# State cross-attention, SiLU MLP and soft mixture of experts in one kernel: the first quarters of w_in laid out half behind half, block 1 moved between quadrants, constant products behind block 8, another order

## The chip, the cores and the metric

The kernel runs on one core of a Trainium2 chip. What counts is the device time of one execution in microseconds (us); the time of a kernel is the median of its runs.

## The reference, cut to what matters

```python
# x: 8 x 8 x 512 x 64, state: 8 x 8 x 32 x 64 (batch, head, rows, depth)
a = softmax(x @ state.T / 8);   xread = a @ state       # tokens read the state
a2 = softmax(state @ x.T / 8);  sread = a2 @ x          # the state reads the tokens
t = concat([xread, sread], rows) -> 4608 tokens x 512   # 8 x (512 + 32) rows

h = t @ w_in                      # 512 -> 2048
t = (h * sigmoid(h)) @ w_out      # 2048 -> 512

logits = t @ phi                  # 32 slots = 8 experts x 4
slot_input = softmax(logits, over tokens).T @ t         # 32 x 512
for e in range(8):                # w1: 512 -> 1024, w2: 1024 -> 512
    slot_out[e] = relu(slot_input[e] @ w1[e]) @ w2[e]
out = softmax(logits, over slots) @ slot_out            # 4608 x 512
```

w_in and w_out come as 64-bit numbers.

## The kernel before

Tokens are worked in nine blocks: blocks 0 to 7 have 512 tokens each (one batch of x), block 8 has the 256 state rows. Lines 1440 to 1750 only describe the work. Every operation is recorded by a `Recorder` (line 280), whose `schedule()` (line 467) plans an order for each engine from a cost model, the due place of each operation, and `RANK` (line 71), a table that shifts the due place of single kinds of operation by numbers; `issue()` (line 628) then issues all. So nearly every instruction has the line L628, and one goes by the names of the tiles.

The first 50 us are the **front**: 64-bit halves of w_in (`raw`, 1 MB each) land and `conv` (line 750) turns each into fp32. The steps are: a first ACTIVATE on ScalarE (ACT) makes the high word (`win<-raw`), a second one on ACT, or one on VectorE (DVE), the low word (`part`), DVE shifts (`TENSOR_SCALAR win`), and DVE or GpSimd (POOL) adds the two (`CUSTOM_DVE_ANT_0 win<-win,part`). `win_half` (line 793) does this for one half (256 columns of each of four 128-row chunks) of one quarter of w_in; a half's results lie in four pieces of 256 in the quarter's tile, so the two halves of a tile lie between one another.

For each block and each quarter of w_in, `wb_mm` (line 950) multiplies the state with that quarter on TensorE (PE): 16 matmuls of 64 rows (`wbp`), whose results are copied into a high and a low part (`wb`, two buffers, ACT, DVE and POOL). The token softmax (`e`, transposed by `eT`) then multiplies it: 16 tiles of hidden units per block (`h`, 6 matmuls each, `hid`, line 1020), SiLU (`g`), and the slot logits (`lg`, 32-column matmuls with w_out·phi, `w2p`). `sc`, `sr` and `srT` are the attention scores and the state's read for the next blocks. On `lg` follow the softmax over tokens (`d`, transposed by `dT`; `lT` transposes the logits) and the products `S` of the slots' weights with all of g (`s_dTg`, line 1259).

g lies for S with tokens on the partitions. DVE transposes each 32x32 square in place. In **moved** blocks (`MOVED`, line 28: blocks 2 to 6) the transposed squares go to one tile, `src`, and 4 DMAs per quarter of h (`by_tokens`, line 1002) carry them into `dst`, 16 DMAs of 256 KB per block; S is then 16 matmuls of 32x512 with all 128 rows, and `dT` is one transposition. In the others (0, 1 and 7) there is no DMA, S is 64 matmuls of 32 rows, and `dT` is four transpositions. Block 0 lies in `src`, block 1 in `dst`.

A scheduler window, `FILL` (line 61), has the planner put **constant products** on TensorE where it plans a gap of the first 60 us: `filler` (line 613) multiplies a tile of ones with itself into a free bank (`lg<-thb 128x256`, two instructions of the profile each). Nobody reads them.

`NATS` (line 22) says at which h of which block one half of w_out is converted and stored for the end (`wo_block`). Behind block 7 come `hid8` and `logits8` (block 8), the slots' sums (`dT`, `siT`, S, `si`), and then the experts: w1 (`f`), w2 (`so`, `sor`), the outputs (`o`). Their 32 weight loads of 1 MB, in `load_w` (line 1342), go from SyncE's queue into 24 `places`, tiles that come free; those in `PIECES` (line 1324) are loaded in four pieces of 256 KB.

Of the kernel before, what the change touches and what calls it, by code (L numbers as in the profile page):

```python
# [24 lines left out]
NATS = {1: {7: 0, 15: 1}, 3: {10: 2}, 4: {10: 3}, 5: {10: 4}, 6: {10: 5}}  # L25
# [5 lines left out]
MOVED = (2, 3, 4, 5, 6)  # L31
# [29 lines left out]
FILL = ((0.0, 60.0),)  # L61
# [10 lines left out]
    ("0", "ACT", "activation", "acc", 0): -711,  # L72
    ("0", "ACT", "activation", "acc", 6): 522,
    ("0", "ACT", "activation", "e", 1): 62,
    ("0", "ACT", "activation", "g", 1): 222,
    ("0", "ACT", "activation", "part", 0): -647,
    ("0", "ACT", "activation", "part", 6): 1417,
    ("0", "ACT", "activation", "win", 0): -724,
    ("0", "ACT", "activation", "win", 3): -17,
    ("0", "ACT", "activation", "win", 6): 1433,  # L80
    ("0", "ACT", "copy", "ar", 0): -198,
    ("0", "ACT", "copy", "e", 2): -428,
    ("0", "ACT", "copy", "e", 7): -578,
    ("0", "ACT", "copy", "wb", 3): 1386,
    ("0", "ACT", "copy", "wb", 5): 1379,
    ("0", "ACT", "copy", "ws", 2): 483,
    ("0", "ACT", "mul", "wp", 0): 1396,
    ("0", "DVE", "reciprocal", "asm", 0): 1500,
    ("0", "DVE", "reciprocal", "asm", 1): 1500,
    ("0", "DVE", "reciprocal", "tm", 0): -319,  # L90
    ("0", "DVE", "reduce_max", "tm", 0): -489,
    ("0", "DVE", "reduce_max", "tm", 1): -39,
    ("0", "DVE", "reduce_max", "tm", 2): 1381,
    ("0", "DVE", "reduce_sum", "tm", 1): -164,
    ("0", "DVE", "reduce_sum", "tm", 2): 1500,
    ("0", "DVE", "tensor_copy", "ss", 1): 643,
    ("0", "DVE", "tensor_scalar", "acc", 0): 1479,
    ("0", "DVE", "tensor_scalar", "acc", 4): -189,
    ("0", "DVE", "tensor_scalar", "acc", 5): -841,
    ("0", "DVE", "tensor_scalar", "asm", 3): 1500,  # L100
    ("0", "DVE", "tensor_scalar", "part", 1): -23,
    ("0", "DVE", "tensor_scalar", "part", 4): -1364,
    ("0", "DVE", "tensor_scalar", "tm", 0): -510,
    ("0", "DVE", "tensor_scalar", "win", 4): 599,
    ("0", "DVE", "tensor_tensor", "acc", 2): -30,
    ("0", "DVE", "tensor_tensor", "ar", 0): -504,
    ("0", "DVE", "tensor_tensor", "s", 0): -359,
    ("0", "DVE", "tensor_tensor", "s", 1): 2,
    ("0", "DVE", "tensor_tensor", "s", 2): 1500,
    ("0", "DVE", "tensor_tensor", "wb", 2): 719,  # L110
    ("0", "DVE", "tensor_tensor", "wb", 3): 387,
    ("0", "DVE", "tensor_tensor", "wb", 5): 1500,
    ("0", "DVE", "transpose", "s", 7): -1129,
    ("0", "DVE", "transpose", "src", 4): 1500,
    ("0", "PE", "matmul", "h", 11): -998,
    ("0", "PE", "matmul", "lg", 8): 1218,
    ("0", "PE", "matmul", "sr", 1): 1500,
    ("0", "PE", "matmul", "wps", 2): -662,
    ("0", "PE", "transpose", "eT", 2): 143,
    ("0", "SP", "dma_start", "phi", 0): 1486,  # L120
    ("0", "SP", "dma_start", "raw", 0): 3,
    ("0", "SP", "dma_start", "raw", 1): -2,
    ("0", "SP", "dma_start", "raw", 2): -4,
    ("0", "SP", "dma_start", "raw", 3): 229,
    ("0", "SP", "dma_start", "raw", 5): 1004,
    ("0", "SP", "dma_start", "raw", 6): 1497,
    ("0", "SP", "dma_start", "ss", 1): 1421,
    ("0", "SP", "dma_start", "xT", 0): -219,
    ("7", "ACT", "activation", "m", 0): 715,
    ("7", "ACT", "copy", "rd", 0): 199,  # L130
    ("7", "ACT", "copy", "wb", 0): -804,
    ("7", "DVE", "scalar_tensor_tensor", "acc", 2): -522,
    ("7", "DVE", "tensor_scalar", "m", 0): -587,
    ("7", "PE", "matmul", "h", 8): 110,
    ("7", "PE", "matmul", "lg", 0): 1500,
    ("7", "PE", "matmul", "lg", 12): 782,
    ("7", "PE", "matmul", "wbp", 1): 1332,
    ("7", "PE", "matmul", "wbp", 2): 488,
    ("8", "ACT", "activation", "cw", 0): 1042,
    ("8", "ACT", "copy", "dT", 1): -521,  # L140
    ("8", "DVE", "tensor_copy", "thb", 1): 272,
    ("8", "DVE", "tensor_scalar", "cm", 1): -1500,
    ("8", "PE", "matmul", "S", 0): 935,
    ("8", "PE", "matmul", "f", 0): -1213,
    ("8", "PE", "matmul", "f", 1): -790,
    ("8", "PE", "matmul", "f", 2): -693,
    ("8", "PE", "matmul", "f", 3): -899,
    ("8", "PE", "matmul", "f", 4): -1500,
    ("8", "PE", "matmul", "f", 5): -905,
    ("8", "PE", "matmul", "f", 6): -907,  # L150
    ("8", "PE", "matmul", "f", 7): -907,
    ("8", "PE", "matmul", "fold", 0): 1351,
    ("8", "PE", "matmul", "h", 0): 1101,
    ("8", "PE", "matmul", "h", 4): 99,
    ("8", "PE", "matmul", "h", 13): 622,
    ("8", "PE", "matmul", "h", 27): 395,
    ("8", "PE", "matmul", "lg", 4): 748,
    ("8", "PE", "matmul", "o", 3): -170,
    ("8", "PE", "matmul", "o", 5): 1500,
    ("8", "PE", "matmul", "o", 7): 420,  # L160
    ("8", "PE", "matmul", "o", 10): 568,
    ("8", "PE", "matmul", "so", 18): -257,
    ("8", "PE", "matmul", "so", 21): 1496,
# [36 lines left out]
    ("m", "DVE", "transpose", "dst", 2): -1188,  # L200
    ("m", "DVE", "transpose", "dst", 3): -1195,
    ("m", "DVE", "transpose", "dst", 5): 1238,
    ("m", "DVE", "transpose", "s", 0): -143,
    ("m", "DVE", "transpose", "s", 1): -68,
    ("m", "DVE", "transpose", "src", 2): -1448,
    ("m", "DVE", "transpose", "src", 3): -1500,
    ("m", "DVE", "transpose", "src", 4): 88,
    ("m", "DVE", "transpose", "src", 6): -1448,
    ("m", "DVE", "transpose", "src", 7): -1408,
    ("m", "PE", "matmul", "S", 0): 692,  # L210
    ("m", "PE", "matmul", "S", 1): 1286,
    ("m", "PE", "matmul", "S", 2): 1500,
    ("m", "PE", "matmul", "h", 1): 1487,
    ("m", "PE", "matmul", "h", 4): 1458,
    ("m", "PE", "matmul", "h", 6): 977,
    ("m", "PE", "matmul", "h", 10): 1104,
    ("m", "PE", "matmul", "h", 13): 889,
    ("m", "PE", "matmul", "lg", 0): 1500,
    ("m", "PE", "matmul", "lg", 1): 1500,
    ("m", "PE", "matmul", "lg", 3): 1500,  # L220
    ("m", "PE", "matmul", "lg", 6): 1064,
# [445 lines left out]
def tile_state_attention_soft_moe(  # L667
# [70 lines left out]
    def raw_at(n):  # L738
        return raws[0][:, n] if n < 4 else raws[1][:, n % 4]
# [280 lines left out]
    def hid(k, j):  # L1020
# [29 lines left out]
        if j == 0 and k < 2:  # L1050
            new_blk(("src", "dst")[k])
# [750 lines left out]
```

## Time and profile before

| | us |
|---|---|
| median of 3 runs | 442.78 (442.65 to 443.43) |
| profiled execution | 443.23 |
| its span | 441.4 |
| around the span | 1.8 |
| TensorE busy | 420.4 |
| VectorE busy | 291.4 |
| ScalarE busy | 284.6 |
| GpSimd busy | 117.6 |

The span runs from the first to the last instruction of the profiled execution. Busy time of TensorE is of pipelined matmuls with modelled ends. In the chain that ended last 84% of the span is TensorE, 6% DMA, 4% ACT.

### The profile page before, as it was taken

The page shows a single profiled execution, that of the slowest core. Times are in us where ns is not written, and L with a number is a line of the kernel's source. Part 1 is how long each engine was busy: PE and PEld are TensorE (multiplying, and loading weights), DVE is VectorE, ACT ScalarE, POOL GpSimd, SP SyncE. Part 2 cuts the span into 40 slices and gives each one's busy share as a digit, 9 for nine tenths or more (in the row PEclk, how much of TensorE's full clock was granted, in tenths as well). Part 3 has the DMA queues.
Part 4 walks back from the last instruction along what each step waited for, and adds up shares of the span by engine and source line. Part 5 has one row for each costly group of instructions (what it writes and reads, how often), then busy time and mean ns, then how long its engine had stood idle before and what let it go on. Part 6 is the DMA issues. An engine that isn't in the chain of part 4 may idle for free.

```text
span 441.4 us, 11019 instructions
## 1 busy us (share of the span) xinstructions
PE 420.4 (95%) x4577; PEld 273.4 (62%) x4577; DVE 291.4 (66%) x547; ACT 284.6 (64%) x512; POOL 117.6 (27%) x71
## 2 busy tenths in 40 slices
PE   7899999999999999999999999999999999999990
PEld 5565657757776775675687567578577684434440
DVE  3999999893797588569668847954865434321461
ACT  4799997757885577679867667766866535011360
POOL 0024332243253223434632511351352220000000
PEclk9999999999999999999999999999999998999996
DMA  8999832224336786998786767347699989999998
GB/s 312 429 423 423 335 145 97 98 97 107 138 143 164 220 262 148 287 316 235 234 227 205 170 204 191 89 120 185 207 415 348 343 318 374 385 425 426 389 329 290
DMA packets 36017, 113.10 MB, mean 256 GB/s; under 512 B 3200, under 2 KB 12288, under 8 KB 28032
## 3 DMA queue, kind: packets, MB, share of 16 engines
q1 hardware_dynamic: 35968, 112.41, 74.7%
q8 instruction: 36, 0.59, 0.5%
q14 instruction: 13, 0.11, 0.1%
HBM read 79.37 MB, written 12.06 MB: 207 GB/s over the span
## 4 chain that ended last, share of the span: by engine, by line
PE 84%; DMA 6%; ACT 4%; DVE 2%; issue 2%; SPq 0%; DVEq 0%
PE h L628 45%; PE S L628 8%; PE lg L628 7%; PE wbp L628 6%; DMA phi<-in_phi_dram 4%; PE so L628 3%; PE f L628 3%; DMA raw<-in_w_in_dram 2%; PE o L628 2%; PE eT L628 1%; PE sr L628 1%; PE sc L628 1%; PE gt L628 1%; ACT part L628 1%; PE w2ps L628 1%
## 5 line engine op out<-in xcount | busy, mean ns | idle before, releaser
L628 PE MATMUL h<-ar,wb 128*128 128x512 f32 x768 | 190.3, 400 | 0.5 <-ACT g L628 0.5
L628 PEld LDWEIGHTS h<-ar,wb 128*128 128x128 f32 x768 | 140.0, 188 | 48.6 <-ACT g L628 8.3
L628 DVE STREAM_TRANSPOSE src<-g 128x512 f32<-128x512 f32 x112 | 76.5, 698 | 24.0 <-ACT g L628 20.1
L628 ACT ACTIVATE g<-h 128x512 f32<-128x512 f32 x100 | 59.1, 609 | 25.9 <-PE h L628 19.7
L628 POOL TENSOR_TENSOR wb<-wf,wb 128x512 fp32r<-128x512 f32 x26 | 33.7, 1296 | 50.8 <-ACT wb L628 31.1
L628 POOL TENSOR_TENSOR s<-s,tm 128x1024 f32<-128x1024 f32 x12 | 23.3, 1938 | 69.3 <-DVE tm L628 19.8
L628 PEld LDWEIGHTS lg<-g,w2p 128*32 128x32 f32 x1056 | 27.2, 109 | 17.7 <-issue 12.8
L628 PE MATMUL lg<-g,w2p 128*32 128x128 f32 (+1 forms) x1056 | 37.0, 279 | 0.0
L628 ACT CAST wb<-wbp 128x512 fp32r<-128x512 f32 x64 | 35.4, 596 | 2.3 <-PE wbp L628 1.5
L628 PE MATMUL wbp<-win,ss 64*32 64x512 f32 x512 | 33.9, 599 | 1.5 <-DVE win L628 1.5
L628 DVE TENSOR_TENSOR wb<-wbp,wb 128x512 fp32r<-128x512 f32 x38 | 25.4, 676 | 12.4 <-ACT wb L628 12.2
L628 ACT ACT_TABLE_LOAD x21 | 26.9, 1283 | 1.1 <-PEq L1792 0.7
L628 DVE SCALAR_TENSOR_TENSOR g<-thb,h 128x512 f32<-128x512 f32 x28 | 18.6, 682 | 13.3 <-ACT thb L628 6.1
L628 ACT ACTIVATE thb<-h 128x512 f32<-128x512 f32 x30 | 18.0, 600 | 13.1 <-PE h L628 13.0
L628 PE MATMUL S<-dst,dT 128*32 128x512 f32 (+1 forms) x296 | 25.3, 608 | 0.0
L628 DVE SCALAR_TENSOR_TENSOR acc<-acc,m,S 128x512 f32<-128x512 f32 x28 | 20.1, 737 | 7.6 <-PE S L628 7.3
L628 PE MATMUL h<-wc,rd 128*128 128x512 f32 x96 | 24.1, 402 | 0.0
L628 PE MATMUL lg<-thb 128*128 128x256 f32 x80 | 20.7, 408 | 1.2 <-DVE thb L628 1.2
L628 POOL TENSOR_TENSOR src<-src 128x1024 uint32<-128x1024 uint32 x6 | 14.4, 2393 | 24.3 <-DVE src L628 24.3
L628 PEld LDWEIGHTS h<-wc,rd 128*128 128x128 f32 x96 | 17.5, 188 | 4.8 <-issue 1.0
L628 PEld LDWEIGHTS lg<-thb 128*128 128x128 f32 x80 | 15.7, 204 | 7.5 <-issue 4.2
L628 DVE TENSOR_REDUCE tm<-s 128x32 f32<-128x1024 f32 (+1 forms) x18 | 19.5, 1090 | 0.3 <-ACT s L628 0.2
(185 smaller groups left out, 604.6 us busy)
## 6 DMA issues: line engine op xcount, KB each, us to landing
dst<-src SPq DMA_DIRECT2D x80, 256.0 KB, 4.5
place<-in_w_dram SPq DMA_DIRECT2D x12, 1024.0 KB, 8.9
xT<-in_xT_dram SPq DMA_DIRECT2D x8, 1024.0 KB, 6.2
raw<-in_w_in_dram SPq DMA_DIRECT2D x8, 1024.0 KB, 10.6
raw<-in_w_outT_dram SPq DMA_DIRECT2D x8, 1024.0 KB, 8.2
xk<-in_xk_dram SPq DMA_DIRECT2D x8, 1024.0 KB, 7.4
src<-in_w_out_dram SPq DMA_DIRECT2D x6, 1024.0 KB, 7.2
dst<-in_w_dram SPq DMA_DIRECT2D x6, 1024.0 KB, 8.5
```

Source lines behind the costliest of these rows:

```text
L628: made = [call(*args, **kwargs) for call, args, kwargs in op.calls]
```

## The change

- `win_c` and `win_half`: quarters 0 and 1 of w_in (`BY_HALVES`) are laid out half behind half, 1024 numbers of a row each, so that each half is contiguous. `wb_mm` and `split_w` read a chunk as two pieces of 256.
- Block 1 is a moved block: it goes through `src` and 16 DMAs to `dst`; block 0 now lies in `dst` from the beginning.
- The halves of w_out in `NATS` are converted at other places.
- A second window of constant products, planned between 355 and 383 us, from the constants' tile `cst`.
- `('w', 1)`, the place of w_in's quarter 1, is loaded in one piece.
- `RANK` has other entries: 160 before, 118 now, 7 of them unchanged.

```diff
-NATS = {1: {7: 0, 15: 1}, 3: {10: 2}, 4: {10: 3}, 5: {10: 4}, 6: {10: 5}}
+NATS = {2: {13: 0}, 3: {10: 1}, 4: {10: 2}, 5: {6: 3, 14: 4}, 6: {10: 5}}
...
-MOVED = (2, 3, 4, 5, 6)
+BY_HALVES = (0, 1)
+MOVED = (1, 2, 3, 4, 5, 6)
...
-FILL = ((0.0, 60.0),)
+FILL = ((0.0, 60.0), (355.0, 383.0))
...
 RANK = {
-    ("0", "ACT", "activation", "acc", 0): -711,
+    ("0", "ACT", "activation", "acc", 2): -323,
...
-        out, v = self.tiles[name][:, 0:256], self.filling[0]
+        out, v = self.tiles[name][:, 0:256], self.filling[0 if start < 100 else 2]
...
+    def win_c(fq, c):
+        t = win_t[fq]
+        if fq not in BY_HALVES:
+            return t[:, c].rearrange("p (h f) -> p h f", h=2)
+        return t.rearrange("p c f -> p (c f)").rearrange("p (h c f) -> p c h f", h=2, c=4)[:, c]
+
     def win_half(fq, half):
         n = halves.index(("win", fq, half))
-        conv(raw_at(n), win_t[fq][:, :, 256 * half:256 * half + 256], share(half), n)
+        t = win_t[fq]
+        if fq in BY_HALVES:
+            t = t.rearrange("p c f -> p (c f)").rearrange("p (h c f) -> p c h f", h=2, c=4)[:, half]
+        else:
+            t = t[:, :, 256 * half:256 * half + 256]
+        conv(raw_at(n), t, share(half), n)
...
-                        rhs=win_t[fq][64 * h2:64 * h2 + 64, c, cols],
+                        rhs=win_c(fq, c)[64 * h2:64 * h2 + 64],
...
-        t = bufs["dst" if k == 1 else "src"]
+        t = bufs["dst" if k == 1 or (k == 0 and 1 in MOVED) else "src"]
...
-            new_blk(("src", "dst")[k])
+            new_blk(("src", "dst")[(k + (1 in MOVED)) % 2])
...
-        t, w = wc[n // 2 % 2][:, n % 2], win_t[fq][:, c]
+        t, w = wc[n // 2 % 2][:, n % 2].rearrange("p z (h f) -> p z h f", h=2), win_c(fq, c)
...
-    PIECES = (('w', 1), ('w', 2), ('w', 3))
+    PIECES = (('w', 2), ('w', 3))
...
-    nc.filling = thb[:, 0, 0:256], 1.5
+    nc.filling = thb[:, 0, 0:256], 1.5, cst[:, 0:256]
```

ScalarE in the front, from the first token softmax (`e_90`) to the first copies of `wb`, before; `win_78` is quarter 0 of w_in, `win_79` quarter 1, `raw` the landed halves, and the words in brackets are the semaphores waited for:

```order
L628 ACTIVATE e_90,asm_92<-e_90,asm_92 128x512 [waits DVE_49,Activation_49]
L628 ACTIVATE win_78<-raw_76 128x4x256 [waits DMAHW5_49,DVE_49]
L628 ACTIVATE part<-raw_76,ulps 128x1024
L628 COPY e_90<-eT_0_99 128x512 [waits PE_49]
L628 ACTIVATE acc<-raw_77 128x1024 [waits DMAHW6_49]
L628 ACTIVATE win_79<-raw_76 128x4x256 [waits DMAHW3_49]
L628 ACTIVATE part<-raw_76,ulps 128x1024 [waits DVE_49]
L628 CAST wb_94<-wbp_0_0_95 128x512 [waits PE_49]
```

The same place now:

```order
L588 ACTIVATE e_90,asm_92<-e_90,asm_92 128x512 [waits DVE_49,Activation_49]
L588 ACTIVATE win_78<-raw_76 128x1024 [waits DMAHW3_49]
L588 ACTIVATE part<-raw_76,ulps 128x1024
L588 ACTIVATE win_79<-raw_76 128x1024 [waits DMAHW5_49]
L588 ACTIVATE part<-raw_76,ulps 128x1024 [waits DVE_49,Activation_49]
L588 COPY e_90<-eT_0_99 128x512 [waits PE_49]
L588 ACTIVATE e_90,asm_92<-e_90,asm_92 128x512
L588 CAST wb_94<-wbp_0_1_96 128x512 [waits PE_49]
```

The second half of quarter 0 (`win_78`) waits for its landing alone, no longer for DVE too; quarter 1's first half comes directly behind it, and a conversion of w_out (`acc`) has gone from between.

TensorE in block 3, from `h_7` to `h_9`, before; `wbp` from `win_81` is this block's last quarter of w_in:

```order
L628 MATMUL h_7_367<-ar_298,wb_343 128x512 x6
L628 MATMUL lT_341<-cst,ls_337 128x128
L628 MATMUL S_0_0_362<-dst,dT_339 32x512 x4
L628 MATMUL lg_355<-g_2_348,w2p 32x128 x4
L628 MATMUL lg_355<-g_3_350,w2p 32x128 x4
L628 MATMUL lg_355<-g_4_352,w2p 32x128 x4
L628 MATMUL S_0_1_363<-dst,dT_339 32x512 x4
L628 MATMUL S_1_0_364<-dst,dT_339 32x512 x4
L628 MATMUL S_1_1_365<-dst,dT_339 32x512 x4
L628 MATMUL wbp_0_0_376<-win_81,ss 32x512 x4
L628 MATMUL wbp_0_1_377<-win_81,ss 32x512 x4
L628 MATMUL h_8_370<-ar_298,wb_356 128x512 x6
```

The same place now; `wbp` from `win_78` is the next block's first quarter:

```order
L588 MATMUL lT_341<-cst,ls_337 128x128
L588 MATMUL lg_355<-g_0_333,w2p 32x128 x4
L588 MATMUL S_0_0_362<-dst,dT_339 32x512 x4
L588 MATMUL S_0_1_363<-dst,dT_339 32x512 x4
L588 MATMUL lg_355<-g_1_335,w2p 32x128 x4
L588 MATMUL lg_355<-g_2_348,w2p 32x128 x4
L588 MATMUL S_1_0_364<-dst,dT_339 32x512 x4
...
L588 MATMUL wbp_0_0_376<-win_81,ss 32x512 x4
L588 MATMUL wbp_0_1_377<-win_81,ss 32x512 x4
L588 MATMUL wbp_0_0_392<-win_78,ss 32x512 x4
L588 MATMUL wbp_0_1_393<-win_78,ss 32x512 x4
L588 MATMUL h_8_370<-ar_298,wb_356 128x512 x6
```

More `lg` stand at this place, and two quarters' `wbp` stand together where one stood.

TensorE behind block 8, before; `lg8s` are block 8's logits, `thb` their exponentials, `siT` and `si` the slots' inputs:

```order
L628 MATMUL lg8t<-lg8s,cst 128x256
L628 MATMUL dT_741<-cst,lg8s 128x32 x2
L628 MATMUL dT_741<-cst,thb 128x32 x2
L628 MATMUL siT_749<-accX,r4e 32x128 x4
L628 MATMUL siT_750<-accX,r4e 32x128 x4
L628 MATMUL S_0_0_745<-dst,dT_742 32x512 x2
...
L628 MATMUL siT_752<-thb,r4e 32x128 x4
L628 MATMUL si<-wo_680,slotT 32x512
```

The same place now:

```order
L588 MATMUL lg8t<-lg8s,cst 128x256
L588 MATMUL dT_741<-cst,lg8s 128x32 x2
L588 MATMUL S_0_0_745<-cst 128x256
L588 MATMUL dT_741<-cst,thb 128x32 x2
L588 MATMUL siT_749<-accX,r4e 32x128 x4
L588 MATMUL siT_750<-accX,r4e 32x128 x4
L588 MATMUL S_0_0_745<-dst,dT_742 32x512 x2
...
L588 MATMUL siT_752<-thb,r4e 32x128 x4
L588 MATMUL f_1_0_764<-cst 128x256
L588 MATMUL si<-wo_680,slotT 32x512
```

Two constant products are added, one between the two groups of `dT`, one ahead of `si`; the rest keeps its order.

## Rows read from the trace of the kernel before

**Rows 1.** Windows: length, busy (x count) PE, PEld, DVE, ACT, POOL; clock, DMA share, GB/s.
```profile
20.00:30.00 10.00, 9.16 (x107) 7.11 (x100) 8.98 (x17) 9.97 (x15) 0.26 (x1) 1.00 1.01 422
...
240.00:250.00 10.00, 10.00 (x73) 5.34 (x72) 9.69 (x22) 7.38 (x16) 4.47 (x4) 1.00 0.45 108
```
**Rows 2.** Chain of waits, 240 to 300 us: start, us, engine, tile, count.
```profile
242.88 3.57 PE S L628 x32
246.45 1.02 PE wbp L628 x16
...
256.03 0.86 PE sc L628 x16
...
272.98 1.59 PE h L628 x6
...
274.68 1.39 PE h L628 x6
```
**Rows 3.** TensorE, 10 to 40 us: start, us, tile, idle before.
```profile
18.96 1.09 PE L628 MATMUL wbp<-win,ss 64*32 64x512 f32 x16 [1.48 <-DVE win L628]
...
24.51 3.01 PE L628 MATMUL h<-ar,wb 128*128 128x512 f32 x12
27.45 1.10 PE L628 MATMUL sr<-xk,e 128*32 128x64 f32 x64
28.56 1.66 PE L628 MATMUL h<-ar,wb 128*128 128x512 f32 x6
```
**Rows 4.** ScalarE, then VectorE, 12 to 20 us.
```profile
15.36 1.14 ACT L628 ACTIVATE win<-raw 128x1024 f32<-128x1024 f32 x1 [1.18 <-DVE win L628]
...
17.68 1.22 DVE L628 CUSTOM_DVE_ANT_0 win<-win,part 128x2048 uint16<-128x2048 uint16 x1 [0.37 <-ACT part L628]
```
**Rows 5.** Costliest groups of the page: busy, mean ns, idle before.
```profile
L628 POOL TENSOR_TENSOR wb<-wf,wb 128x512 fp32r<-128x512 f32 x26 | 33.7, 1296 | 50.8 <-ACT wb L628 31.1
...
L628 ACT CAST wb<-wbp 128x512 fp32r<-128x512 f32 x64 | 35.4, 596 | 2.3 <-PE wbp L628 1.5
...
L628 PE MATMUL lg<-thb 128*128 128x256 f32 x80 | 20.7, 408 | 1.2 <-DVE thb L628 1.2
```
**Rows 6.** Chain of waits, 85 to 150 us and 196 to 204 us.
```profile
88.31 0.44 PE dT L628 x4
...
90.25 4.39 PE S L628 x121
...
136.52 1.88 PE wbp L628 x32
...
201.09 0.11 PE dT L628
```
**Rows 7.** TensorE behind block 8.
```profile
371.93 0.30 PE L628 MATMUL dT<-cst,thb 32*128 32x32 f32 x2 [0.75 <-ACT thb L628]
...
372.77 1.91 PE L628 MATMUL S<-dst,dT 128*32 128x512 f32 x8
...
377.81 0.81 PE L628 MATMUL si<-wo,slotT 128*32 128x512 f32 x2 [0.18 <-DVE slotT L628]
```
**Rows 8.** Window behind block 8, columns as in rows 1.
```profile
373.00:374.00 1.00, 1.00 (x8) 0.21 (x4) 0.79 (x6) 0.26 (x1) 0.00 (x0) 0.50 0.99 418
```
**Rows 9.** Windows of the end, columns as in rows 1.
```profile
362.00:364.00 2.00, 2.00 (x10) 1.63 (x9) 0.00 (x0) 0.60 (x1) 0.00 (x0) 1.00 0.30 99
...
424.00:426.00 2.00, 1.82 (x24) 0.73 (x19) 1.86 (x6) 1.42 (x5) 0.00 (x0) 1.00 0.84 274
...
428.00:438.00 10.00, 2.64 (x32) 1.07 (x31) 3.38 (x10) 2.91 (x10) 0.00 (x0) 0.81 1.08 376
```
**Rows 10.** DMA issues of 380 to 400 us: count, KB each, median us to landing.
```profile
src<-in_w_dram SPq DMA_DIRECT2D x2, 1024.0 KB, 19.9
```
**Rows 11.** SyncE's issue of these two loads; TensorE's first use of them.
```profile
393.15 2.82 SPq L628 DMA_DIRECT2D src<-in_w_dram  x2
...
419.38 1.91 PE L628 MATMUL so<-src 128*32 128x256 f32 x32
```

More of the change, by code (lines that the diff above doesn't have):

```diff
@@ L71 @@
 RANK = {
-    ("0", "ACT", "activation", "acc", 0): -711,
[L73 to L82, printed above, removed]
@@ L128 @@
[L128 to L139, printed above, removed]
@@ new lines @@
+    ("0", "ACT", "activation", "e", 1): 524,
+    ("0", "ACT", "activation", "g", 1): 1403,
+    ("0", "ACT", "activation", "g", 11): 802,
+    ("0", "ACT", "activation", "part", 6): 1498,
+    ("0", "ACT", "activation", "win", 6): 1500,
+    ("0", "ACT", "copy", "wb", 0): -822,
+    ("0", "ACT", "copy", "wb", 1): -1041,
+    ("0", "ACT", "copy", "wb", 5): 1500,
+    ("0", "ACT", "copy", "ws", 1): -581,
+    ("0", "ACT", "mul", "wp", 0): 1292,
+    ("0", "DVE", "reciprocal", "tm", 0): 1500,
+    ("0", "DVE", "reduce_max", "asm", 0): 5,
@@ new lines @@
+    ("0", "DVE", "reduce_max", "tm", 3): 1496,
+    ("0", "DVE", "reduce_sum", "mask", 0): 1322,
+    ("0", "DVE", "reduce_sum", "tm", 2): 1500,
+    ("0", "DVE", "tensor_scalar", "acc", 5): -720,
+    ("0", "DVE", "tensor_scalar", "part", 1): -248,
+    ("0", "DVE", "tensor_scalar", "part", 4): -1500,
+    ("0", "DVE", "tensor_scalar", "srs", 0): 1500,
+    ("0", "DVE", "tensor_scalar", "tm", 2): -665,
+    ("0", "DVE", "tensor_scalar", "win", 1): 1500,
+    ("0", "DVE", "tensor_scalar", "win", 2): 1500,
@@ new lines @@
+    ("0", "DVE", "tensor_scalar", "win", 3): -309,
+    ("0", "DVE", "tensor_tensor", "acc", 2): -1192,
+    ("0", "DVE", "tensor_tensor", "wb", 1): 1500,
+    ("0", "DVE", "tensor_tensor", "wb", 2): 363,
+    ("0", "DVE", "tensor_tensor", "wb", 3): 31,
+    ("0", "DVE", "tensor_tensor", "wb", 5): 1500,
+    ("0", "DVE", "transpose", "dst", 4): 1500,
+    ("0", "DVE", "transpose", "dst", 10): -158,
+    ("0", "DVE", "transpose", "dst", 11): -1055,
+    ("0", "DVE", "transpose", "s", 7): 373,
+    ("0", "PE", "matmul", "sr", 1): 1454,
@@ new lines @@
+    ("7", "PE", "matmul", "lg", 15): 1481,
+    ("7", "PE", "matmul", "wbp", 0): 1433,
+    ("8", "ACT", "copy", "dT", 1): -217,
+    ("8", "DVE", "reciprocal", "fin", 0): 876,
+    ("8", "DVE", "tensor_copy", "dst", 0): 648,
+    ("8", "DVE", "tensor_copy", "place", 4): -83,
+    ("8", "DVE", "tensor_copy", "place", 6): -1375,
+    ("8", "DVE", "tensor_copy", "place", 7): -1500,
+    ("8", "DVE", "tensor_copy", "thb", 1): 28,
+    ("8", "DVE", "tensor_copy", "thb", 3): -412,
+    ("8", "DVE", "tensor_reduce", "fin", 0): 1500,
@@ new lines @@
+    ("8", "PE", "matmul", "o", 6): -701,
+    ("8", "PE", "matmul", "o", 7): -363,
+    ("8", "PE", "matmul", "so", 20): -72,
+    ("8", "PE", "matmul", "so", 21): -63,
+    ("8", "PE", "matmul", "so", 22): -138,
+    ("8", "PE", "matmul", "so", 23): -91,
+    ("8", "PE", "matmul", "so", 27): -739,
+    ("8", "PE", "matmul", "so", 31): -504,
+    ("8", "PE", "transpose", "gt", 3): -60,
+    ("8", "PE", "transpose", "gt", 5): 403,
+    ("m", "ACT", "activation", "g", 6): -400,
+    ("m", "ACT", "copy", "wb", 3): 1212,
```

187 lines of the change are left out of this document (57 added, 130 removed).

## The prediction

> **What bounds the kernel now.** I read the busy table first (TensorE 95%), then the chain of waits, then windows, and only then the engines' timelines at the places where the chain leaves TensorE. In the middle, from about 50 to 360 us, TensorE is the path: a window of ten microseconds there is filled with ten of matmuls at full granted clock, with DMA at 0.45, though VectorE is nearly full too [rows 1]. The chain of the same stretch is one TensorE piece after another without a hole, so what a matmul group costs there can be read from its piece [rows 2]. In the front the path is landing, conversion and softmax: ScalarE and the DMA are full from 20 to 30 us [rows 1], and TensorE stands between its groups, 1.48 us of it ahead of the first `wbp` [rows 3]; what it does meanwhile is partly constant products, 80 records of 408 ns, two for each of 40 [rows 5]. Behind block 8 TensorE's granted clock falls to 0.50, the lower level, 1.2 GHz [rows 8], after idle stretches of which 0.75 us is the longest [rows 7]. From 364 us the DMA is full but for a few places, and the last ten microseconds are stores [rows 9].
>
> **The front.** Before, the first step of quarter 0's second half waits 1.18 us on ScalarE for VectorE's add of the first half, since the halves lie between one another; the second half's add then waits for ScalarE's low word, which follows that step [rows 4]. Half behind half the step can begin with its landing, at 14.2 instead of 15.4. The low word then ends about 1.2 earlier, VectorE's add begins at 16.6 instead of 17.7, and `wbp` at 17.9 to 18.0 instead of 18.96. That is 0.9 to 1.1 earlier. Behind it, `sr` (1.10 us) stood between the first two `h` tiles and the third, which began at 28.56 [rows 3]; now it stands ahead of `h_0`, in time that was waited for. `h_0` then begins about 23.5 (24.51 before), and the third tile at 27.45, where `sr` began. I carry the front's gain on at 1.2. Lower bound zero: the DMA is full here [rows 1], and the landings of quarter 1 and of w_out, which the change doesn't make earlier, may be late next. Upper bound 2.1: 1.0 of the wait and 1.1 of `sr`. The order has 36 constant products there instead of 40; the planned holes that went with them are the same time, and aren't added again. I take 1.2, as the third `h` tile follows both effects at once.
>
> **Block 1.** S takes 4.39 us in a block that isn't moved [rows 6], 3.57 in a moved one [rows 2]: 0.82 less. The four transpositions of `dT` become one: 0.44 less 0.11 [rows 6], 0.33. Instead there are 16 more DMAs of 256 KB; in block 3's stretch those of a moved block lie in a DMA share of 0.45 [rows 1], and SyncE queues nothing behind them that block 1 or 2 waits for soon. I cost them at nothing. If the last landing were late, S would be put off behind it; as bound I take the whole 1.15 that the move saves. Reading w_in's quarters in two pieces of 256 I cost at nothing: S of a moved block, which reads pieces of 128, takes 0.45 for a round of four that lie beside each other (3.57 by 8), `sc`, in one piece, 0.43 for a round of eight (0.86 by 2) [rows 2]. As bound, 0.02 for two rounds in each of 18 groups, 0.7.
>
> **Order in the middle.** A group costs more when the shape of the array changes ahead of it: six matmuls of `h` take 1.59 us after `sr` or `wbp`, 1.39 otherwise, and 16 of 64 rows take 1.02 as `wbp` behind another shape, 0.86 as `sc` behind one of their own [rows 2]. So 0.16 to 0.20 a change. I counted the changes by the new order between the first `lg` of block 0 and block 8's transpositions: 87 where there were 96, by grouping `lg` with S and two quarters' `wbp` with each other, as the pieces of the order show. Nine by 0.16 is 1.44 us. Lower bound zero, if a group placed together waits for its data; upper bound 1.8 by 0.20.
>
> A rule bears on this, in the Trainium skill, "TensorEngine Tiling (Array Packing)", section Key Properties: a change of the tiling mode makes TensorE drain. The trace agrees, with the 0.16 and 0.20 above. By it the two constant products behind block 8 are two more pairs of changes; the sum below charges one, since the first stands in an idle stretch.
>
> **The clock behind block 8.** S of block 8 comes in two groups of eight records, one of which took 1.91 us [rows 7] with the clock at 0.50 [rows 8]; the second is like it and begins a little before the first ends: I take 3.6 for both. The 32 records of a moved block take 3.57 at full clock [rows 2], 16 take 1.79. So 1.8 us stand there if the clock stays up. What fell ahead of it is idle time: the longest 0.75 us, ahead of the second group of `dT`. The first new constant product goes into exactly this place. The second stands ahead of `si`, in 0.18 of idle [rows 7], and costs a change (0.16) and what it reaches beyond that idle time, 0.23 (408 ns [rows 5] less 0.18). Gain if it holds: 1.8 − 0.16 − 0.23, 1.4. Bounds: a loss of 0.4 (the clock falls all the same and the products delay `si`), a gain of 1.8.
>
> **The end.** If TensorE comes earlier by the sum, do DMAs let it? The last two loads of w2 are issued from 393.15 to 395.97 [rows 11] and take 19.9 [rows 10]: they land at 413 to 416, and are first read at 419.38 [rows 11], 3.4 us later. The DMA has holes before that: the window from 362 to 364 moves 99 GB/s instead of 376 as in the stores' stretch, and the one from 424 to 426 has a share of 0.84 against 1.08 [rows 9]. The first is a wait for free places, so an earlier block 7 brings all loads forward with it; the front's and the middle's gains pass. The clock's gain comes behind the hole and draws on the 3.4 of slack and the later holes. The place of w_in's quarter 1, loaded whole instead of in pieces, can begin its load only when all of it is free; the first hole, 0.70 of two microseconds or 1.4 us, has room for that. I take it at nothing, and 1.4 as bound.
>
> **Sum**: 1.2 + 0.82 + 0.33 + 1.44 + 1.4 = 5.19. From the profiled execution's own time of 443.23, 438.0. The median of the runs is 0.45 lower than that execution, which I leave inside the range. Its own range is 436.2 to 439.6: more by the front's 0.9 and the changes' 0.4, less by the front's 1.2 and a part of the middle's changes.
>
> **Rivals.**
> *The clock falls again.* One constant product doesn't fill 0.75 us (two records of 408 ns, half beside each other), and the idle 0.18 and the narrow `dT` and `siT` groups stay. Then 1.4 becomes a loss of about 0.1: 443.23 − 3.79 + 0.1 = 439.5. For it: little is added; against: it sits where the longest hole was. Chance 0.22.
> *The middle's savings aren't on the path.* TensorE's ends are modelled, and VectorE is busy 9.69 of 10 in the same stretch [rows 1]; if VectorE paces, then 0.82, 0.33 and 1.44 (2.6) turn into idle TensorE: 443.23 − 2.6 = 440.6, and 441.8 if the front's 1.2 is given back too at the landings. Against it: the chain without holes [rows 2]. Chance 0.18. A rule of the Trainium skill speaks for this one, in "Trainium Kernel Development and Optimization", Performance Expectations: matmul busy time is a bad measure of nearness to the limit, as matmuls are pipelined. The chain of this case, where a shape change shows as 0.16, speaks against it.
> *Slower: the banks held by `wbp`.* In blocks 2 to 6 the next block's first quarter of `wbp` now stands directly behind this block's last one, ahead of `h_8`. Its `wb` tile is one of two, and still read until `h_11`. Its results stay in their banks till then; copies can begin only behind, and `eT` and others want the banks. Behind `h_11` stand `h_12` to `h_14` (three by 1.39) and an `sc` (1.02), 5.2 us, until something needs what was copied. The copies take two casts and one copy of 0.6 on ScalarE and one operation of 1.3 on POOL [rows 5], 3.1 in a row. It decides from the point where ScalarE begins more than 2.1 us late, five times over: stalls of 1.3 each make 443.23 − 5.19 + 6.5 = 444.5. Against it: block 2 of before has 32 `wbp` together (1.88 us) [rows 6], with nothing idle behind. Chance 0.11.
> *It doesn't do what it says*: the holes in the front move to the landings, changes cost nothing there, the clock falls, block 1 waits for its DMAs: 442.8. Chance 0.04.
>
> **Numbers.** The forecast has 0.45, clock again 0.22, middle 0.18, slower 0.11, none 0.04. A measurement tells 0.2% here (0.9 us) from no change. Faster by more: 0.45 + 0.22 + three quarters of 0.18 = 0.80; within: the rest of 0.18 and 0.04, 0.09; slower 0.11. The range of 436.0 to 442.2 takes in the clock's case and the middle's and leaves out the slower one and the front's last tenths.
>
> **What would show it.** First `wbp` at 18.0 and the third `h` tile near 27.5; ScalarE's second `win` step without a wait for VectorE. S of block 1 in 3.6 us, one `dT`. No holes in the chain from 50 to 360 us, whose stretch from the first `h` to `top` is shorter by 2.6. A granted clock of 1.00 in the windows of block 8's S and 8 records in 0.9. It is wrong if TensorE shows idle time ahead of `h_12` to `h_0` in blocks 2 to 6, if the clock row still has 0.50, or if the last loads of w2 land just ahead of their `so`.

## The result and the profile after

The changed kernel takes 438.63 us in the median of 6 runs (437.55 to 440.12), the kernel before 443.05 in 6 runs beside it: a ratio of 0.9906, 95% interval 0.9881 to 0.9932. Forecast were 438.0 and a range of 436.0 to 442.2. Faster was right and the size nearly so, but not each term of the sum: the clock's came to nothing or nearly, the front's depends on the execution, and the middle's came out near the forecast (2.5 of 2.6). One execution among the experiments below, of the kernel before with the products alone, took 831.54 us and is left out.

The execution profiled first is the slowest of the six, 440.12, with a span of 438.3 (before 441.4). TensorE in the front of the changed kernel; columns as in rows 3, the bracket is the idle time ahead and what ended it:

```profile
17.98 1.09 PE L588 MATMUL wbp<-win,ss 64*32 64x512 f32 x16 [0.43 <-DVE win L588]
...
23.39 3.03 PE L588 MATMUL h<-ar,wb 128*128 128x512 f32 x12
...
28.54 1.66 PE L588 MATMUL h<-ar,wb 128*128 128x512 f32 x6 [1.68 <-ACT g L588]
...
39.56 3.12 PE L588 MATMUL h<-ar,wb 128*128 128x512 f32 x12
```

`wbp` and `h_0` come where they were forecast (18.0 and 23.5), 1.0 and 1.1 earlier than in [rows 3]; the third `h` tile does not. It stands at 28.54, where it was, behind a new wait of 1.68 us for the first SiLU. What held that is seen on ScalarE, 14 to 29 us:

```profile
14.16 1.16 ACT L588 ACTIVATE win<-raw 128x1024 f32<-128x1024 f32 x1
...
25.45 1.12 ACT L588 ACTIVATE win<-raw 128x1024 f32<-128x1024 f32 x1 [0.99 <-DMA raw<-in_w_in_dram]
26.59 1.28 ACT L588 ACT_TABLE_LOAD   x1
27.89 0.60 ACT L588 ACTIVATE g<-h 128x512 f32<-128x512 f32 x1
```

The second step of quarter 0 begins at 14.16, without the 1.18 of [rows 4]: the layout does what it says. But ScalarE then waits 0.99 for the landing of quarter 1's second half, and the table load and the first SiLU stand behind it.

TensorE behind block 8, after (answers to [rows 7, 8]):

```profile
367.66 0.70 PE L588 MATMUL lg8t<-lg8s,cst 128*128 128x256 f32 x2 [0.18 <-ACT lg8s L588]
...
368.56 0.68 PE L588 MATMUL S<-cst 128*128 128x256 f32 x2
369.47 0.30 PE L588 MATMUL dT<-cst,thb 32*128 32x32 f32 x2 [0.23 <-ACT thb L588]
...
370.31 1.74 PE L588 MATMUL S<-dst,dT 128*32 128x512 f32 x8
...
375.56 0.62 PE L588 MATMUL si<-wo,slotT 128*32 128x512 f32 x2
```

and the windows there and up to the end; the last line is the same window of the kernel before:

```profile
356.00:364.00 8.00, 8.00 (x52) 6.58 (x54) 2.49 (x4) 2.35 (x6) 1.62 (x2) 1.00 0.59 197
...
371.00:372.00 1.00, 1.00 (x12) 0.36 (x8) 0.22 (x2) 0.00 (x0) 0.00 (x0) 0.50 1.05 442
...
366.00:434.00 68.00, 58.46 (x702) 26.86 (x694) 24.53 (x69) 18.32 (x52) 0.00 (x0) 0.96 1.03 399
366.00:434.00 68.00, 61.17 (x724) 27.70 (x722) 26.56 (x72) 19.83 (x55) 0.00 (x0) 0.97 1.01 390
```

The idle time of 0.75 has become 0.23, and the granted clock falls to 0.50, the 1.2 GHz level, all the same. From 366 to 434 the DMA has a share of 1.03, against 1.01 before; the hole that before had at 424 us [rows 9] is gone (1.06 from 424 to 426).

Two new waits stand in the middle. One is in block 4, where the second of two `wbp` that stand together waits for a bank:

```profile
206.94 1.09 PE L588 MATMUL wbp<-win,ss 64*32 64x512 f32 x16
208.62 1.09 PE L588 MATMUL wbp<-win,ss 64*32 64x512 f32 x16 [0.59 <-DVE acc L588]
```

The other stands ahead of the first `wbp` behind the fifth `h` tile, and waits for VectorE's add of another quarter of w_in. In the kernel before, four records of constant products fill this place (first line); now two do, and TensorE is idle for 0.60 (second line):

```profile
42.33 1.02 PE L628 MATMUL lg<-thb 128*128 128x256 f32 x4
...
43.71 1.09 PE L588 MATMUL wbp<-win,ss 64*32 64x512 f32 x16 [0.60 <-DVE win L588]
```

Block 1's `dT` and S, in the chain of waits of the changed kernel; before they took 0.44 and 4.39 [rows 6]:

```profile
125.62 0.11 PE dT L588
...
127.58 1.72 PE S L588 x16
...
130.39 1.72 PE S L588 x16
```

The gain of this execution by stretches: front −0.06 (the fifth `h` tile at 39.50 before, 39.56 now), from there to `lg8t` 2.52, from `lg8t` to `si` −0.21, behind that 0.85; in all 3.1.

### The profile page after: what moved, and what is told of

Read it like the earlier page. It is cut to its first block, busy times and chain, and to the rows that moved or that the text cites. A ratio compares the mean times of both kernels' runs of the same rounds, so it can differ in the third digit from the quotient of the medians.

```text
span 438.3 us, 10843 instructions
## 1 busy us (share of the span) xinstructions
PE 416.2 (95%) x4474; PEld 272.9 (62%) x4474; DVE 290.6 (66%) x548; ACT 286.0 (65%) x514; POOL 118.5 (27%) x71
## 4 chain that ended last, share of the span: by engine, by line
PE 79%; DMA 8%; ACT 6%; DVE 3%; issue 1%; SPq 1%; DVEq 0%
PE h L588 42%; PE lg L588 7%; PE S L588 7%; PE wbp L588 6%; DMA raw<-in_w_in_dram 4%; PE so L588 3%; PE f L588 3%; DMA src<-in_w_out_dram 2%; PE o L588 2%; PE sc L588 1%; PE eT L588 1%; PE sr L588 1%; ACT L588 1%; DMA ss<-in_stT_dram 1%; ACT g L588 1%
## 5 line engine op out<-in xcount | busy, mean ns | idle before, releaser
L588 DVE STREAM_TRANSPOSE src<-g 128x512 f32<-128x512 f32 x112 | 78.1, 704 | 36.9 <-ACT g L588 34.9
L588 PE MATMUL S<-dst,dT 128*32 128x512 f32 (+1 forms) x328 | 29.1, 604 | 0.0
L588 PE MATMUL h<-wc,rd 128*128 128x512 f32 x96 | 24.3, 401 | 0.0
L588 PE MATMUL lg<-thb 128*128 128x256 f32 x72 | 19.6, 417 | 1.2 <-DVE thb L588 1.2
L588 DVE TENSOR_REDUCE asm<-e 128x2 f32<-128x1024 f32 x8 | 9.7, 1208 | 15.4 <-ACT e L588 15.4
L588 PEld LDWEIGHTS lg<-thb 128*128 128x128 f32 x72 | 14.1, 206 | 6.5 <-issue 3.4
```

The source lines that it names most:

```text
L588: made = [call(*args, **kwargs) for call, args, kwargs in op.calls]
```

## The experiments

Two theories stood after this profile. *Theory 1*: the clock behind block 8 holds in some executions and falls in others, and the products decide it; that would be most of the way from 3.1 in this profile to 4.4 in the median. *Theory 2*: the products do nothing. Later ones are named where they come.

**The changed kernel again**, unchanged.

> The changed kernel once more, for runs beside the next three. Two theories of the 4.4 us that the median fell. Theory 1 (the clock behind block 8 holds in some executions and falls in others): the runs fall into two groups, some with a mean granted clock of 0.989 to 0.990 and a span about 1.5 us longer than those with 0.992 to 0.993; the profile of the first look was of the first group. Median 438 to 438.8, ratio 0.990. Theory 2 (the constant products behind block 8 do nothing for the time, all of the gain is in the middle and the end): the clock and the span of the runs have nothing to do with each other; the spread is that of the kernel before.

438.76 (437.65 to 440.6), ratio 0.9912 (0.989 to 0.9934). Its profile, TensorE:

```profile
27.24 1.67 PE L588 MATMUL h<-ar,wb 128*128 128x512 f32 x6 [0.62 <-ACT g L588]
...
366.70 0.70 PE L588 MATMUL lg8t<-lg8s,cst 128*128 128x256 f32 x2 [0.18 <-ACT lg8s L588]
...
369.36 1.07 PE L588 MATMUL S<-dst,dT 128*32 128x512 f32 x8
...
373.38 0.62 PE L588 MATMUL si<-wo,slotT 128*32 128x512 f32 x2
```

The same instructions: here the clock held (8 records in 1.07 instead of 1.74), and the third `h` tile came at 27.24, near the forecast's 27.45. But the two groups of runs that theory 1 expected aren't there: a run of 440.6 has a mean clock of 0.991, one of 438.8 has 0.989. That mean also counts the idle end, so it doesn't tell the theories apart.

**Without the second window of constant products**, twice.

```diff
-FILL = ((0.0, 60.0), (355.0, 383.0))
+FILL = ((0.0, 60.0),)
```

> The changed kernel without the second window of constant products; the order of everything else is the same. Theory 1: the clock falls in every execution, mean clock 0.988 to 0.989, and the median is 1.0 to 1.7 us above the changed kernel's, about 439.8; in the profile S behind block 8 takes 3.6 us and the idle time ahead of the second dT group is about 0.75. Theory 2: within 0.5 us of the changed kernel, or faster by 0.2, since a product and a change of shape less stand ahead of si.

> The changed kernel without the second window once more, to tell it from the changed kernel (438.7 in eleven runs). Theory D: the products and the clock that they were to hold are worth nothing at the end, since the DMA is full behind them: 438.0 to 438.8, whatever the clock does in S behind block 8, and the profile's end is 69.9 to 70.7 us behind lg8t whether the clock falls or not. Theory 1 as it was (the clock decides): above 439 in at least half of the runs.

438.11 (ratio 0.9893, 0.9876 to 0.9910) and 438.68 (0.9907, 0.9883 to 0.9930): with the products or without, the medians can't be told apart. Two profiles of it, the first with a clock that held and the second with one that fell, TensorE behind block 8:

```profile
368.05 0.31 PE L588 MATMUL dT<-cst,thb 32*128 32x32 f32 x2 [0.75 <-ACT thb L588]
...
368.88 1.06 PE L588 MATMUL S<-dst,dT 128*32 128x512 f32 x8
...
372.52 0.82 PE L588 MATMUL si<-wo,slotT 128*32 128x512 f32 x2 [0.18 <-DVE slotT L588]
```

```profile
369.16 1.60 PE L588 MATMUL S<-dst,dT 128*32 128x512 f32 x8
...
373.89 0.81 PE L588 MATMUL si<-wo,slotT 128*32 128x512 f32 x2 [0.18 <-DVE slotT L588]
```

The 0.75 us of idle time stands ahead of a clock that held, and in the first profile of the changed kernel the clock fell behind 0.23. So the products don't decide it, and theory 1 falls.

**More constant products** behind block 8 (seven instead of two).

```diff
-                n = int((st - at - (0.2 if fills else 2.2)) / FILLER)
+                n = int((st - at - (0.2 if fills else 2.2) + (0.5 if at > 100 else 0.0)) / FILLER)
```

> The changed kernel with more constant products behind block 8: one more ahead of lg8t, two instead of one between the dT groups, one ahead of siT, two instead of one ahead of si, one behind si. Theory 1: with less idle time ahead of S the clock holds in all or nearly all executions, mean clock 0.992 to 0.994; the products cost up to 0.5 us of order, the clock gives back 1.8 in the executions where it fell; median 437.3 to 438.0, and a smaller spread. Theory 2: slower than the changed kernel by 0.3 to 0.8 us, whatever the clock does.

438.73 (0.9917, 0.9901 to 0.9933): no gain. The clock held in its profile, and `si` came at 374.69, later than in the two profiles above with a clock that held (373.38 and 372.52).

**The products alone**, in the kernel before.

```diff
-FILL = ((0.0, 60.0),)
+FILL = ((0.0, 60.0), (355.0, 383.0))
```

> The kernel before with the second window of constant products alone; it puts the same two products at the same places. Theory 1: some executions keep the clock: the median is 0.5 to 1.5 us below before's, and the mean clock of those that keep it 0.991 or more. Theory 2: no change within 0.5 us.

441.92 in 11 runs against 442.56 beside it, 0.9988 (0.9975 to 1.0002): no change that can be told, as theory 2 had it. The last matmul of `si` starts 9.78 us behind `lg8t` (371.34) in its profile, first line; in the kernel before, profiled again below, it is 9.77 behind (371.26), second line:

```profile
381.12 0.59 PE L628 MATMUL si<-wo,slotT 128*32 128x512 f32 x1
...
381.03 0.59 PE L628 MATMUL si<-wo,slotT 128*32 128x512 f32 x1
```

In both the clock held.

**The layout undone** in the changed kernel; the order stays.

```diff
-BY_HALVES = (0, 1)
+BY_HALVES = ()
```

> The changed kernel with the first quarters of w_in laid out as before (each half in four pieces of 256); the order on every engine stays. Theory A (the layout is what makes the front earlier): ScalarE's second step for quarter 0 waits 1.2 us for VectorE again, the first wbp comes at 18.9 to 19.1 instead of 17.7 to 18.1, the third h tile at 28.3 to 28.6, the fourth quarter's first h after it (39.3 to 39.7) up to 1.0 later than in the changed kernel's second look (38.64); median 0.5 to 1.0 us slower. Theory B (the landing of quarter 1's second half at 24.1 to 25.5 us decides the front, with the table load and the first SiLU behind it on ScalarE): wbp later by 1, but the third h tile within 0.3 of 27.2 to 28.6 for the like landing, and the median within 0.3 us of the changed kernel.

438.71 (0.9908, 0.9892 to 0.9924): the median doesn't tell it from the changed kernel. TensorE, 15 to 40 us:

```profile
18.98 1.09 PE L588 MATMUL wbp<-win,ss 64*32 64x512 f32 x16 [1.36 <-DVE win L588]
...
28.69 1.66 PE L588 MATMUL h<-ar,wb 128*128 128x512 f32 x6 [0.62 <-ACT g L588]
...
39.75 2.42 PE L588 MATMUL h<-ar,wb 128*128 128x512 f32 x9
```

With its landing at 24.0, as early as in the second profile of the changed kernel, the third `h` tile is 1.45 later than there and the fifth 1.1 later (38.64 there). So theory A holds for the stretch where the landing is early; where it is late (25.4, the first profile) the third tile stood at 28.54 with the new layout too, and theory B holds. That the layout is worth anything in the median is not shown.

**The pairs of `wbp` taken apart** in the changed kernel. Theory M: each change of shape costs its share on the path.

```diff
 RANK = {
+    ("m", "PE", "matmul", "wbp", 3): 600,
```

> The changed kernel with the next block's first wbp no longer directly behind this block's last one, but later, two to five tiles of h behind (one number of the order's table added). From the first lg to block 8 the shape of the array changes 104 times instead of 87. Theory M (each change costs 0.16 us on the path): the stretch from the fifth h tile of block 0 to lg8t, 328.1 us in the changed kernel with one wait of 0.6 in it, becomes 17 x 0.16 = 2.7 us longer, less the 0.6 where that wait goes; median 2.0 to 2.8 us slower, about 441. Theory V (VectorE or ScalarE paces the middle, changes are hidden): within 0.5 us of the changed kernel. Theory W (the pairs hold banks and cost waits): 0.5 us or more faster.

441.75 (0.9967, 0.9949 to 0.9986): 3.0 slower than the changed kernel, theory M's sign, and a little over its size; V and W fall. In its profile the stretch from the fifth `h` tile to `lg8t` is 330.44, 2.3 longer than in the changed kernel, and the part behind `lg8t` is 71.1 us long against 70.7 and 70.3: so not all of the 3.0 stands where the changes do. The chain of waits at the last quarter of block 5 (start, us, tile), here and in the changed kernel's first profile:

```profile
244.11 4.34 PE h L588 x18
248.45 1.02 PE wbp L588 x16
249.47 2.96 PE h L588 x12
252.43 1.02 PE wbp L588 x16
253.45 4.33 PE h L588 x18
```

```profile
244.91 1.88 PE wbp L588 x32
246.79 9.82 PE h L588 x42
```

Two `wbp` and 48 `h` cost 13.67 where apart. In one piece they cost 1.88, and the 42 `h` behind cost 9.82; six more by the same rate are 1.40, so 13.10. That is 0.57 for the three changes more, 0.19 each. Over the whole stretch from the fifth `h` tile to `lg8t`, less its idle time, this kernel takes 2.6 us more than the two profiles of the changed kernel, and 2.9 to 3.1 more than the three of it without the second window, which have the same order there. For 17 changes that is 0.15 to 0.18 each.

**Block 1 moved alone**, in the kernel before, with the halves of w_out at the new places.

```diff
-MOVED = (2, 3, 4, 5, 6)
+MOVED = (1, 2, 3, 4, 5, 6)
-NATS = {1: {7: 0, 15: 1}, 3: {10: 2}, 4: {10: 3}, 5: {10: 4}, 6: {10: 5}}
+NATS = {2: {13: 0}, 3: {10: 1}, 4: {10: 2}, 5: {6: 3, 14: 4}, 6: {10: 5}}
```

> The kernel before with block 1 as a moved block alone (block 0 in dst, the halves of w_out at their new places); the table of the order stays. S has 48 and dT 3 records fewer, but by the order that comes out the shape changes 106 times instead of 96. Theory M: 0.82 + 0.33 less for block 1, 10 x 0.16 = 1.6 more for the changes: the stretch from the fifth h tile to lg8t is 0.4 us longer than before's 330.6, the median 0 to 0.6 us slower. Theory V (changes cost nothing, block 1's saving is all that counts): 1.15 us shorter, median about 441.4. If block 1's DMAs come late: a wait ahead of S of block 1.

447.48, slower by 1.07% (1.0107, 1.0083 to 1.0131). Both theories miss. TensorE shows what neither counted:

```profile
64.27 0.66 PE L628 MATMUL eT<-cst,e 128*128 128x128 f32 x4 [1.16 <-ACT e L628]
...
95.47 0.66 PE L628 MATMUL dT<-cst,d 128*128 128x128 f32 x4 [0.31 <-DVE ss L628]
96.80 0.33 PE L628 MATMUL lT<-cst,ls 128*128 128x128 f32 x1 [0.68 <-ACT dT L628]
```

In the stretch of the middle, 4.6 longer than before, 2.4 are idle time, 1.1 more constant products and 1.0 more in `lg`. S of block 1 itself takes 3.57 (1.00 and 2.57 in the chain of waits), the 0.82 less that was forecast; over all blocks S is 0.7 shorter. The waits shown are for ScalarE and VectorE, whose work for blocks 0 and 1 comes too late for TensorE with the old table. A wait of S for block 1's DMAs isn't among them.

**The new table alone**, in the kernel before.

```diff
 RANK = {
-    ("0", "ACT", "activation", "acc", 0): -711,
+    ("0", "ACT", "activation", "acc", 2): -323,
...
```

> The kernel before with the new table of the order alone: block 1 isn't moved, the layout, the window and the pieces are the old ones. By the order that comes out the shape of the array changes 97 times from the first lg to block 8 (96 before, 87 in the changed kernel, where the table met block 1 moved). Theory M (S's records, changes of shape at 0.18 each and waits make the middle's time): nothing of the 3 us is there: the stretch from the fifth h tile to lg8t within 1.0 us of before's 330.6 apart from waits; median 442.3 to 444. Theory O (the searched order is worth the time by itself, whatever it orders): median 440.5 or less.

445.7, slower by 0.69% (1.0069, 1.0049 to 1.0089). Theory O falls; M's count is right in that nothing of the gain is there, but it didn't foresee 2.4 us more in the middle. TensorE has them as constant products (0.8 more) and waits (1.7 more):

```profile
48.97 1.99 PE L586 MATMUL wbp<-thb 128*128 128x256 f32 x8
...
73.35 1.07 PE L586 MATMUL w2ps<-acc,phi 128*32 128x512 f32 x8 [0.74 <-DVE acc L586]
75.85 1.08 PE L586 MATMUL w2q<-cst,w2s 128*128 128x32 f32 x8 [0.56 <-ACT w2s L586]
```

So each part alone loses, where the changed kernel without the new layout (438.71) or without the second window (438.11 and 438.68) keeps all of its gain.

**Quarter 1's second half loaded earlier**, in the changed kernel.

```diff
-    ("0", "SP", "dma_start", "raw", 3): 411,
+    ("0", "SP", "dma_start", "raw", 3): -1400,
```

> The changed kernel with the second half of w_in's quarter 1 loaded ahead of two halves of w_out instead of behind them (one number of the table); the order of the front changes with it. Theory B: its landing comes at 19 to 20.5 instead of 24.1 to 25.5, ScalarE's table load and first SiLU no longer wait for it, and the third h tile follows the two before it and sr, at 26.5 to 27.3, in every execution; whether the fifth h tile is earlier too (before 38.6 to 39.6) depends on w_out's halves, now later: between 1.0 us faster and 0.5 slower in the median. Theory A: the third h tile stays where it was, since the landing isn't what it waits for.

444.32 (1.0036, 1.0022 to 1.0050), far outside both expectations. It landed at 19.0, and the third `h` tile still came at 28.27, for reasons that are in the trace: `sr` went back behind the first two tiles, the first SiLU on ScalarE now stood behind another conversion, and the first `sc` took 1.96 us in this execution instead of 1.09, which alone is 0.9. The time was lost later, TensorE:

```profile
34.37 8.90 PE L588 MATMUL lg<-thb 128*128 128x256 f32 x40
42.92 0.82 PE L588 MATMUL h<-ar,wb 128*128 128x512 f32 x2
43.98 1.19 PE L588 MATMUL h<-ar,wb 128*128 128x512 f32 x4 [0.24 <-DVE wb L588]
```

Twenty constant products cover a hole of 8.9 us: the fifth `h` tile needs a low part of `wb` that VectorE finished last, behind the next block's softmax. One load moved, and the planner's order turned against the path elsewhere. It says little on the landing by itself.

**The place loaded in pieces again**, without the second window.

```diff
-FILL = ((0.0, 60.0), (355.0, 383.0))
+FILL = ((0.0, 60.0),)
-PIECES = (('w', 2), ('w', 3))
+PIECES = (('w', 1), ('w', 2), ('w', 3))
```

> The changed kernel without the second window of constant products and with the place of w_in's quarter 1 loaded in four pieces again. Theory D (from 364 us to the end the DMA is full, and only what starts the loads earlier is worth time): the first piece goes out before the stop for free places at 359 to 362, part of the DMA's hole from 356 to 364 (a mean share of 0.6 in the changed kernel) is filled, and the end comes up to 0.5 us earlier than without this edit; median 437.5 to 438.1. Theory N (the hole is a wait for places that pieces don't free): no change, 438.0 to 438.3.

437.74 (0.9898, 0.9873 to 0.9923), the lowest median of all, 1.02% below before; from the changed kernel it isn't told apart, as the intervals overlap. Its DMA share from 356 to 364 is 0.74 where the changed kernel's first profile has 0.59, but 0.78 without the pieces too, in the profile with a clock that held: theory D isn't shown by it.

**The kernel before again**, one run.

> The kernel before once more, for a second profile. The stretch from the fifth h tile to lg8t is 330.6 us within 0.3, as in the two profiles with its order so far; the front moves by up to 1.3 us with the landings. If the clock holds in S behind block 8, S and si come 1.2 to 1.4 us earlier with no product there; the end comes earlier by at most that.

442.81. TensorE:

```profile
6.59 1.96 PE L628 MATMUL sc<-xT,ss 64*32 64x512 f32 x16 [1.59 <-DMA ss<-in_stT_dram]
...
20.15 1.09 PE L628 MATMUL wbp<-win,ss 64*32 64x512 f32 x16 [1.38 <-DVE win L628]
...
371.26 0.70 PE L628 MATMUL lg8t<-lg8s,cst 128*128 128x256 f32 x2 [0.18 <-ACT lg8s L628]
...
373.91 1.07 PE L628 MATMUL S<-dst,dT 128*32 128x512 f32 x8
...
377.41 0.81 PE L628 MATMUL si<-wo,slotT 128*32 128x512 f32 x2 [0.18 <-DVE slotT L628]
```

The clock held with no product there; the front is 1.2 later than in [rows 3], as the first `sc` took 1.96 instead of 1.09. The stretch of the middle is 330.58, as before.

## Why the prediction was right, step by step

The starts of the same instructions in the profiles, in us; "clock" is that of S behind block 8:

| kernel, profile | fifth h | to lg8t | clock | lg8t to si | si to end |
|---|---|---|---|---|---|
| before, 1 | 39.50 | 330.62 | fell | 7.69 | 63.6 |
| before, 2 | 40.68 | 330.58 | held | 6.15 | 63.5 |
| before + products | 40.72 | 330.62 | held | 6.53 | 63.2 |
| changed, 1 | 39.56 | 328.10 | fell | 7.90 | 62.8 |
| changed, 2 | 38.64 | 328.06 | held | 6.68 | 63.6 |
| no second window, 1 | 39.25 | 326.98 | held | 6.29 | 63.8 |
| no second window, 2 | 39.18 | 327.32 | fell | 7.39 | 62.8 |
| the same with pieces | 38.85 | 327.08 | held | 6.29 | 63.7 |

**The front (1.2).** The mechanism was right up to the third `h` tile, and the rival bound too. `wbp` comes 1.0 earlier and `sr` costs nothing. What is late next, in some executions, is the landing of quarter 1's second half, which the lower bound named. But the gain was carried on from the third tile, and the fifth is where the middle begins. It stands at 39.50, 40.68 and 40.72 in the three profiles of before's front, at 38.64 to 39.70 in seven of the changed one (five in the table, 39.70 with more products, 39.41 with `wbp` apart). The means, 40.3 and 39.2, don't compare like with like: the first `sc` took 1.96 us instead of 1.09 in two of the three and in one of the seven (39.41). Where it took 1.09 the gain is 0.3 (39.50 against a mean of 39.2), where it took 1.96 it is 1.3 (40.7 against 39.41), each with a single profile on one side. So 1.2 isn't shown.

**Block 1 and the order in the middle (0.82 + 0.33 + 1.44).** The stretch is 2.5 us shorter in the two profiles of the changed kernel, which have the wait of 0.6 in block 4, and 3.3 to 3.6 in the three with 0.2 of that wait or none; forecast was 2.6. To see in what, I gave each TensorE record the time to the next one's start, less idle time, and summed by tile, for the first profile of before and the last row of the table (3.54 shorter):

- S −1.62, `dT` −0.92, but `lT` and `srT` +1.26, as they now stand next to other shapes: −1.28
- `h`, `lg`, `wbp`, `sc`, `sr`, `gt`: −1.86; `top` +0.07
- constant products behind the fifth `h` tile: −1.13, one instead of three
- idle time: +0.66

The last two belong together: 0.60 of the idle time stands where products stood (the wait at 43.71 above), so a hole has only lost part of its filling, and 0.47 is what is left of both. The matmuls that are read give 3.1, and 2.7 in the two profiles of the changed kernel itself, where forecast were 2.6. The sums by tile don't part block 1 from the order: with the new table alone, and block 1 as before, S is 0.50 and `dT` 0.41 shorter and `lT` and `srT` 1.20 longer. Block 1 is seen by itself: its S takes 3.57 where it alone is moved and 3.44 in the changed kernel, against 4.39, its `dT` 0.11 in the changed kernel against 0.44. A change of shape cost 0.15 to 0.18 where 17 were put back; the forecast had 0.16 to 0.20.

So TensorE's path is what is spent in the middle, and the rival that the savings aren't on the path fell: with 17 changes put back the stretch is 2.3 us longer, though it has less idle time.

**The clock (1.4).** This is the step that failed. Of six profiles with these two products the clock fell in two, of seven without any in three: the 0.75 of idle time doesn't decide it, and the products don't prevent it. What does decide it is open. The products put the first `si` 0.4 later (6.53 and 6.68 against 6.15 and 6.29), as was charged for them, but `si`'s last matmul starts no later (9.77 and 9.78 behind `lg8t`), so that behind it nothing of that is left. A fall costs 1.1 to 1.5 from `lg8t` to `si`, where the forecast had 1.8. From `lg8t` to the end the kernel before takes 71.3 with the fall and 69.7 without: 1.6. The changed kernel with its products takes 70.7 with the fall and 70.3 without, and without the second window 70.2 against 70.1 and 70.0: 0.4 and less. Profiles with a clock that held differ by more among themselves (69.8 with more products, 71.1 with `wbp` apart), so there a clock that holds isn't told from nothing. That the DMA takes the rest is not shown: its share from 366 to 434 us is 1.03 in the changed kernel, but it is 1.01 and 1.02 in the two profiles of the kernel before, where the fall cost 1.6. The rival "the clock falls again" (439.5) described the profiled execution, but its reason, idle time that stays, isn't what decides: the clock held behind all 0.75 of it.

**The end.** Nothing was expected. The hole that before had at 424 us [rows 9] is gone, and the profiled execution was 0.85 shorter behind `si`; where the clock held, the end is no shorter than before's. Which edit closed it, the table's new order of `so` and `o` or the earlier start, wasn't tried by itself.

**The slower rival** shows one trace of itself: the wait of 0.59, in one of five blocks and not in every execution. It ends with VectorE's sums of S (`acc`), so it is read as a wait for a bank that they give back, not for the `wb` tile. Its price of 1.3 in each block wasn't met.

The sum as the profiles give it: between the two first ones, both with a clock that fell, 3.1 (front −0.1, middle 2.5, behind `lg8t` 0.6); between the two second ones, both with a clock that held, 4.0 (front 2.0, of which 0.9 is the first `sc`, middle 2.5, behind `lg8t` −0.6). Measured were 4.4 between the medians, forecast 5.19. The middle is in every pair; the rest changes with the execution, and nothing in the profiles stands in for the clock's 1.4. That the total came so near is in part luck.

## What to carry over

Where the chain of TensorE has no holes, count the changes of array shape and the records, and pay for each from the row of the same tile in the other surroundings: 0.16 us each held up (0.15 to 0.18) when 17 of them were put back. Before paying for a clock that holds, profile the same kernel several times: here it held and fell with the gap ahead of it and with the gap filled, and at the end of the changed kernel it was worth 0.4 us or less, where 1.4 had been forecast. Compare starts only between executions whose earlier steps took the same time. And a part of a searched whole can lose when applied alone: block 1 moved cost 1.07%, the new table 0.69%, both together with the rest gained 0.94%.

## What the runs showed of the hardware that I had not expected

- The granted clock behind the same instructions and the same idle time holds in one execution and falls to 0.50, the 1.2 GHz level, in the next: it fell in 3 of 7 profiles with an idle time of 0.75 us, in 2 of 6 with 0.23 or 0.24. The Trainium skill, "TensorE: Matmul & The Clock Gate", Part 1, says of a kernel's start that the number of its slow matmuls varies from run to run; here it is seen in the middle of a kernel.
- The first `sc`, 16 matmuls, takes 1.09 us in some executions and 1.96 in others of the same kernel, with a granted clock of 1.00 in the windows of both; the front moves by 0.9 to 1.2 with it. What it is stays open.
- The tenth load of the front lands at 23.9 to 24.3 us or at 25.3 to 25.5, with nothing between, in both kernels.
